# V's products moved between the two groups of a trip's second quarter, in a one-core decode block (attention and feed-forward) on Trainium2

## Chip, core and metric

The kernel runs on one core of one Trainium2 chip. The metric is device time in microseconds (us) of one execution; lower is better. Three executions of the kernel before were timed (median 298.16 us), and a fourth was recorded with the hardware profiler. The engines are called PE (TensorE), DVE (VectorE), ACT (ScalarE), POOL (GpSimd) and SP (SyncE, which issues all large loads here). PEld is PE's weight load.

## The reference, cut to what matters

One decode step for B = 2 sequences, D = 640, 32 heads with head size 192, a key and value cache of 8192 tokens of which the last W = 2048 are used, and a gated feed-forward of width 1536:

```
x = A_x
q = layernorm(x) @ wq
k = k_cache[:, :, Sk - W:, :]
v = v_cache[:, :, Sk - W:, :]
scores = einsum("bhqd,bhkd->bhqk", q, k) * Dh ** -0.5
o = einsum("bhqk,bhkd->bhqd", softmax(scores), v)
h = x + o @ wo
h2 = h + (gelu(layernorm(h) @ w_gate) * (layernorm(h) @ w_up)) @ w_down
```

There is one query per sequence and head, so every key and value is read once and used once: 16 loads of 6.29 MB (8 of K, 8 of V) beside the weights.

## The kernel before, in words

**Storage.** A ring in on-chip memory has three slots of 49152 bytes per partition. A load of K or V (named k0 to k7 and v0 to v7) is one quarter of one sequence's window: 512 tokens for all 32 heads, 128 partitions with 128 tokens each, and fills one slot. Even K loads and v7 use slot 0, odd K loads (and `wq` before them) slot 1, v0 to v6 slot 2. So V has one slot alone: v1 can't be loaded before all reads of v0 are done. `wo` comes into slots 2 and 1 at the end, the feed-forward weights into slots 1 and 0.

**Order of loads.** `load` puts every load into one list, in the order wg0, wq, k0, k1, v0, k2, v1, k3, v2, k4, v3 and so on to v6, v7, wo0 to wo3, the rest. `pump` (called by `done`, when the last reader of a slot has been written into the program) takes them strictly in that order. SP runs them as one queue: each DMA waits until the readers of what lay in its slot have finished, and whatever stands behind it waits too.

**Groups and trips.** The work is 16 groups (g), each half a load. A trip J of the loop (4 trips, looped on PE and DVE, unrolled on ACT and POOL) takes groups 4J to 4J+3: the first quarter (4J and 4J+1) reads load k(2J), the second quarter (4J+2 and 4J+3) reads k(2J+1). For a group:
- `transposes` (L549 to L571): PE transposes K through four PSUM banks, 48 instructions (L560); DVE (L571) and ACT (L569) copy the banks out;
- `scores` (L613 to L622): 24 matmuls (L618) into one bank;
- `softmax` (L626 to L634): DVE takes minus the maximum (L628, L629), ACT the exponentials (L633);
- `e_turn` (L656) and `e_blocks` (L659): DVE turns the exponentials and spreads them into `eblk`, the stationary operand of V's products;
- `pv` (L665 to L683): 64 matmuls (L673) of `eblk` with V, even groups into bank `ops`, odd ones into `m1`. V's load v(2J) belongs to groups 4J and 4J+1, v(2J+1) to 4J+2 and 4J+3.

**Where V's products stand.** They run two groups behind. Those of the first quarter, `pv(4J)` and `pv(4J+1)`, stand in the second quarter of the same trip: behind `maxima()`, that is behind both groups' transposes and scores (L792 to L794). In the program `pv` then has DVE copy the bank to `osb` (L682, L683). Those of the second quarter, `pv(4J+2)` and `pv(4J+3)`, stand in `behind` (L695) in the next trip's first quarter, behind both groups' scores; after the last trip they stand by themselves. After a second quarter `sums` (L643) and `combine` (L685) work out the weights by which partial results are joined; PE's matmuls for it are L644, L687 and L688. In trip 2 `heads_done(0)` (L707) follows `behind`.

Each engine runs its program in order, and all waits are on semaphores; the tables `R`, `W` and `X` of an operation say what it reads, writes, and which PSUM bank it uses.

Of the kernel before, what the change touches and what calls it, by code (L numbers as in the profile page):

```python
# [16 lines left out]
DH = 192  # L17
# [229 lines left out]
def bass_sequential_preLN__sliding_block_cached__geglu_ffn__decode_kernel(  # L247
# [12 lines left out]
    with ExitStack() as ctx:  # L260

        def sb(name, shape, dt):
            return ctx.enter_context(nc.sbuf_tensor(name, shape, dt))

        def ps(name, shape, dt):
            return ctx.enter_context(nc.psum_tensor(name, shape, dt))
# [62 lines left out]
        osb = sb("osb", [128, 2, DH], F32)  # L329
# [19 lines left out]
        ops_ = ps("ops", [128, 512], F32)  # L349
        m1 = ps("m1", [128, 512], F32)  # L350
# [25 lines left out]
        def done(*keys):  # L376
            used.update(keys)
            pump()
# [36 lines left out]
        def dve(fn, R=(), W=(), X=(), cls=1):  # L415
            return P.op("dve", fn, R, W, X, cls=cls if looped else 0)

        def act(fn, R=(), W=(), X=(), cls=0):
            return P.op("act", fn, R, W, X, cls=cls)

        def pe(fn, R=(), W=(), X=(), cls=0):
            return P.op("pe", fn, R, W, X, cls=cls)
# [126 lines left out]
        def transposes(g, lo, hi):  # L549

            kk, ktoks = where["k", g // 2]
            kv = kk.bitcast(F32)
            for n in range(lo, hi):
                c, ch, scalar = TR[n]
                bank, x = tps[n % 4], ("t", n % 4)

                def fn(e, c=c, ch=ch, bank=bank):
                    for u in range(4):
                        off = 6144 * (g % 2) + 128 * (3 * (4 * ch + u) + c)
                        ins = e.transpose(bank[:, 128 * u:128 * (u + 1)], kv[:, off:off + 128], identf[:, :])  # L560
                    return ins

                pe(fn, R=ktoks + ["identf"], X=[x])
                if g % 2 == 1 and n == 11:
                    done(("k", g // 2))
                src = bank.bitcast(BF16)
                dst = ktr[:, c, 1024 * ch:1024 * (ch + 1)]
                if scalar:
                    act(lambda e, dst=dst, src=src: e.activation(out=dst, in_=src, func=ACT.Copy), W=[("kt", n)], X=[x])  # L569
                else:  # L570
                    dve(lambda e, dst=dst, src=src: e.tensor_copy(dst, src), W=[("kt", n)], X=[x], cls=0)  # L571
# [41 lines left out]
        def scores(g):  # L613
            def fn(e):
                for k in range(6):
                    for hg in range(4):
                        cols = ktr[:, k // 2, :].rearrange("p (a x w) -> p a x w", a=16, w=2)[:, :, 32 * hg:32 * (hg + 1), k % 2]
                        ins = e.matmul(sps[32 * hg:32 * (hg + 1), :], lhsT=rq[:, k, hg, :], rhs=cols, start=(k == 0),  # L618
                                       stop=(k == 5), tile_position=(0, 32 * hg))
                return ins  # L620

            pe(fn, R=[("rq", hg) for hg in range(4)] + [("kt", n) for n in range(12)], X=["s"])  # L622
            if g % 4 == 3 and g + 1 < 4 * NQ:
                q_masked((g + 1) // 8)

        def softmax(g):  # L626
            n = g % 4
            dve(lambda e: e.memset(gate[:, :], 0.0), W=["gate"], X=["s"], cls=0)  # L628
            dve(lambda e: e.tensor_tensor_reduce(  # L629
                out=sm[:, :].rearrange("p (u x) -> p u x", x=32), in0=sps[:, :].rearrange("p (u x) -> p u x", x=32),  # L630
                in1=mska[:, :].unsqueeze(1).to_broadcast([128, 16, 32]), scale=-1.0, scalar=2.0 * BIG, op0=ALU.add, op1=ALU.min,
                accum_out=nms[:, n:n + 1]), R=["mska"], W=["sm", ("nm", n)], X=["s"], cls=0)
            act(lambda e: e.activation(out=eexp[:, :], in_=sm[:, :], func=ACT.Exp, bias=nms[:, n:n + 1], scale=-1.0,  # L633
                                       accum_out=zr[:, n:n + 1]), R=[("nm", n), "sm", "gate"], W=["eexp", ("zr", n)])  # L634

        def maxima():
            dve(lambda e: e.tensor_reduce(out=nmin[:, :], in_=nms[:, :], axis=AX.X, op=ALU.min), R=[("nm", k) for k in range(5)],
                W=["nmin"], cls=0)
            dve(ts(mrhs[:, :], oht[:, :], nmin[:, 0:1], ALU.mult), R=["oht", "nmin"], W=["mrhs"], cls=0)
            act(lambda e: e.activation(out=wz[:, 0:5], in_=nms[:, :], func=ACT.Exp, bias=nmin[:, 0:1], scale=-1.0),  # L640
                R=["nmin"] + [("nm", k) for k in range(5)], W=["wz"])
# [14 lines left out]
        def e_turn(g):  # L656
            dve(lambda e: e.transpose(et[:, :], eexp[:, :]), R=["eexp"] + [("eb", 0, 3)] * (g % 2), W=["et"], cls=0)  # L657

        def e_blocks(g):  # L659
            for hg in range(4):  # L660
                dve(lambda e, hg=hg: e.tensor_copy(eblk[32 * hg:32 * (hg + 1), g % 2, :, hg, :],  # L661
                                                   et[32 * hg:32 * (hg + 1), :].rearrange("p (a x) -> p a x", x=32)),
                    R=["et"], W=[("eb", g % 2, hg)], cls=0)

        def pv(g):  # L665
            vv, vtoks = where["v", g // 2]
            bank, x = ((ops_, "o"), (m1, "m1"))[g % 2]

            def fn(e):
                for a in range(16):  # L670
                    for r in range(4):
                        t = 64 * (g % 2) + 4 * a + r
                        ins = e.matmul(bank[32 * r:32 * (r + 1), 0:DH],  # L673
                                       lhsT=eblk[:, g % 2, a, :, :].rearrange("p s x -> p (s x)")[:, r:128:4],
                                       rhs=vv[:, DH * t:DH * (t + 1)], start=(a == 0), stop=(a == 15),
                                       tile_position=(0, 32 * r), skip_group_check=True)
                return ins

            pe(fn, R=[("eb", g % 2)] + [("eb", g % 2, hg) for hg in range(4)] + vtoks, X=[x])
            if g % 2 == 1:  # L680
                done(("v", g // 2))
            if g % 4 < 2:  # L682
                dve(lambda e: e.tensor_copy(osb[:, g % 4, :], bank[:, 0:DH]), W=[("osb", g % 4)], X=[x], cls=0)  # L683

        def combine():  # L685
            def fn(e):
# [8 lines left out]
        def behind(g):  # L695
            dve(ts(osum[:, :], osum[:, :], wp[:, 4:5], ALU.mult), R=["wp", "osum"], W=["osum"], cls=0)
            for k in range(4):
                if k == 2:
                    pv(g)
                    pv(g + 1)  # L700
                src, tok, x = ((osb[:, 0, :], [("osb", 0)], []), (osb[:, 1, :], [("osb", 1)], []), (ops_[:, 0:DH], [], ["o"]),
                               (m1[:, 0:DH], [], ["m1"]))[k]
                dve(lambda e, k=k, src=src: e.scalar_tensor_tensor(out=osum[:, :], in0=src, scalar=wp[:, k:k + 1], in1=osum[:, :],
                                                                   op0=ALU.mult, op1=ALU.add),
                    R=["wp", "osum"] + tok, W=["osum"], X=x, cls=0)
# [67 lines left out]
        for J in range(4):  # L773
            P.loop_seg("a", J)
            for g in (4 * J, 4 * J + 2):
                transposes(g, 0, 12)
                scores(g)
                softmax(g)
                transposes(g + 1, 0, 12)
                scores(g + 1)  # L780
                e_turn(g)
                softmax(g + 1)
                if g % 4 == 0:
                    if J > 0:
                        P.loop_seg("pa", J)
                        behind(g - 2)
                    if J == 2:
                        P.loop_seg("op", J)
                        heads_done(0)
                    P.loop_seg("a2", J)  # L790
                else:
                    maxima()  # L792
                    pv(g - 2)
                    pv(g - 1)  # L794
                e_blocks(g)
                e_turn(g + 1)
                e_blocks(g + 1)
                if g % 4 == 0:
                    P.loop_seg("b", J)
                else:  # L800
                    sums()
                    combine()
# [55 lines left out]
        def rjb(t):  # L858
# [18 lines left out]
            W=[("osb", 0), ("osb", 1)], X=["o"])  # L877
# [60 lines left out]
```

## Time and profile before

| what | value |
|---|---|
| timed executions | 294.39, 298.24, 298.16 us; median 298.16 us |
| the profiled execution | 294.99 us, of which the span of recorded work is 293.7 us |
| granted TensorE clock, mean of the span | 0.853 |
| busy | PE 188.1 us, PEld 155.5 us, DVE 148.0 us, ACT 95.5 us, POOL 23.0 us |
| DMA | 122.46 MB, mean 417 GB/s over the span |
| SP waiting for PE's last product of V (L673, L644 rows) | 110.1 + 79.0 + 8.7 us in the queue's own waits |

In a timeline a row is: start, duration, engine, line, operation, output and input, number of instructions, and in square brackets how long the engine sat idle before it and what it waited for. In a table of stretches a row is: the stretch, its length, busy time of each engine with the number of instructions, the granted TensorE clock (1.00 is full), the mean busy share of the 16 DMA engines and what they moved.

### The profile page before, as it was taken

What the parts mean: (1) busy time and instruction counts of PE and PEld (TensorE: products, weight loads), DVE (VectorE), ACT (ScalarE), POOL (GpSimd) and SP (SyncE); (2) the same over time, 40 slices, a digit from 0 to 9 for tenths busy, and PEclk for the clock granted to TensorE, in tenths of its full rate; (3) what the DMA queues carried; (4) which work ended last, traced back from release to release, by engine and by line L of the source; (5) the groups of instructions that cost most, each with busy time, mean ns of one, the idle gap of its engine ahead of it and who ended that gap; (6) DMA issues with size and microseconds to landing.
All of it is one profiled execution on the core that took longest, in us unless ns stands there. A gap on an engine that the chain in (4) does not pass through costs nothing.

```text
span 293.7 us, 6215 instructions
## 1 busy us (share of the span) xinstructions
PE 188.1 (64%) x2557; PEld 155.5 (53%) x2557; DVE 148.0 (50%) x365; ACT 95.5 (33%) x128; POOL 23.0 (8%) x69
## 2 busy tenths in 40 slices
PE   2007388678848955884788468847881788365385
PEld 1004286476738745763777367637670776352143
DVE  5000036766665673577266746663675266634022
ACT  1001026536506611471266024612650256100001
POOL 8930200000200000002000000020000000000000
PEclk9999959979977996999599959996997599868555
DMA  8999999999889999999999999999999999999994
GB/s 322 486 425 428 424 428 428 424 418 428 353 321 428 428 430 428 428 428 442 442 455 449 428 428 428 428 442 449 428 428 428 428 428 428 428 389 430 423 416 171
DMA packets 4204, 122.46 MB, mean 417 GB/s; under 512 B 478, under 2 KB 608, under 8 KB 1248
## 3 DMA queue, kind: packets, MB, share of 16 engines
q1 hardware_dynamic: 4188, 122.29, 97.0%
q8 instruction: 8, 0.13, 0.2%
q14 instruction: 4, 0.03, 0.0%
q10 hardware_dynamic: 4, 0.00, 0.0%
HBM read 122.29 MB, written 0.00 MB: 416 GB/s over the span
## 4 chain that ended last, share of the span: by engine, by line
DMA 56%; PE 29%; issue 6%; ACT 3%; DVE 3%; SPq 1%; DVEq 0%
DMA ring<-in_A_k_cache_dram 48%; PE tpp L560 19%; DMA ring<-in_A_wo_dram 9%; PE sps L618 3%; PE m L673 2%; PE ops L673 2%; ACT ktr L569 2%; ACT eexp L633 1%; DVE ktr L571 1%; SPq L374 1%; DVE sm L629 1%; PE sps L837 1%; PE m L886 1%; PE m L738 1%; PE ops L837 1%
## 5 line engine op out<-in xcount | busy, mean ns | idle before, releaser
L560 PE MATMUL tpp<-identf,ring 128*128 128x128 f32 x768 | 107.4, 307 | 36.6 <-DMA ring<-in_A_k_cache_dram 30.5
L560 PEld LDWEIGHTS tpp<-identf,ring 128*128 128x128 f32 x768 | 100.1, 160 | 45.6 <-DMA ring<-in_A_k_cache_dram 31.6
L571 DVE COPY ktr<-tpp 128x1024 bf16<-128x1024 bf16 x112 | 77.0, 691 | 54.8 <-PE tpp L560 53.7
L569 ACT ACTIVATE ktr<-tpp 128x1024 bf16<-128x1024 bf16 x80 | 77.4, 1020 | 75.0 <-PE tpp L560 75.0
L618 PE MATMUL sps<-ktr,rq 128*32 128x512 bf16 x384 | 25.2, 390 | 13.7 <-DVE ktr L571 13.7
L633 ACT ACTIVATE eexp<-sm,nms 128x512 bf16<-128x512 f32 x16 | 11.6, 723 | 41.1 <-DVE nms L629 41.1
L618 PEld LDWEIGHTS sps<-ktr,rq 128*32 128x32 bf16 x384 | 10.3, 94 | 24.0 <-ACT ktr L569 17.5
L434 POOL TENSOR_TENSOR rq<-qs,mask 128x192 bf16<-128x192 bf16 x16 | 7.8, 519 | 167.7 <-PE sps L618 154.7
L629 DVE CUSTOM_DVE_ANT_1 sm<-sps,mska 128x512 f32<-128x512 f32 x16 | 11.0, 687 | 16.4 <-issue 16.3
L661 DVE COPY eblk<-et 32x512 bf16<-32x512 bf16 x64 | 18.2, 284 | 2.0 <-DVE nms L629 0.2
L580 PE MATMUL tpp<-ring,xnT 128*32 128x384 bf16 x80 | 5.3, 443 | 15.3 <-DMA ring<-in_A_wq_dram 15.3
L673 PE MATMUL ops<-ring,eblk 128*32 128x192 bf16 x512 | 13.7, 261 | 2.1 <-DMA ring<-in_A_v_cache_dram 2.1
L673 PEld LDWEIGHTS ops<-ring,eblk 128*32 128x32 bf16 x512 | 12.9, 112 | 3.2 <-DMA ring<-in_A_v_cache_dram 2.2
L687 PE MATMUL m<-wz,rowperm 128*128 128x6 f32 x8 | 2.4, 369 | 17.2 <-DVE wz L434 17.2
L673 PE MATMUL m<-ring,eblk 128*32 128x192 bf16 x512 | 12.7, 249 | 0.0
L580 PEld LDWEIGHTS tpp<-ring,xnT 128*32 128x32 bf16 x80 | 2.9, 127 | 17.4 <-issue 15.4
L657 DVE STREAM_TRANSPOSE et<-eexp 128x512 bf16<-128x512 bf16 x16 | 11.3, 706 | 1.0
L673 PEld LDWEIGHTS m<-ring,eblk 128*32 128x32 bf16 x512 | 11.7, 109 | 0.0
L687 PEld LDWEIGHTS m<-wz,rowperm 128*128 128x128 f32 x8 | 2.0, 312 | 17.6 <-DVE wz L434 17.6
L603 DVE CAST qs<-ops 128x384 bf16<-128x384 f32 x1 | 0.6, 557 | 21.3 <-PE ops L598 21.3
L738 PE MATMUL m<-ring,ot 128*2 128x320 bf16 x96 | 6.3, 423 | 6.6 <-DMA ring<-in_A_wo_dram 6.6
L824 ACT ACTIVATE lnv<-tpp,eps_t 98x1 f32<-98x1 f32 x1 | 0.3, 261 | 28.4 <-PE tpp L822 28.4
(144 smaller groups left out, 101.3 us busy)
## 6 DMA issues: line engine op xcount, KB each, us to landing
ring<-in_A_k_cache_dram SPq DMA_DIRECT2D x8, 6144.0 KB, 34.9
ring<-in_A_v_cache_dram SPq DMA_DIRECT2D x8, 6144.0 KB, 22.4
ring<-in_A_wq_dram SPq DMA_DIRECT2D x1, 7680.0 KB, 21.3
ring<-in_A_wo_dram SPq DMA_DIRECT2D x4, 1920.0 KB, 19.2
ring<-in_B_w_gate_dram SPq DMA_DIRECT2D x1, 1536.0 KB, 28.7
ring<-in_B_w_up_dram SPq DMA_DIRECT2D x1, 1536.0 KB, 31.9
ring<-in_B_w_down_dram SPq DMA_DIRECT2D x1, 960.0 KB, 25.5
ring<-in_B_w_down_dram SPq DMA_DIRECT2D x1, 480.0 KB, 26.4
```

Source lines behind the costliest of these rows:

```text
L434: return lambda e: e.tensor_tensor(out=out, in0=a, in1=b, op=op)
L560: ins = e.transpose(bank[:, 128 * u:128 * (u + 1)], kv[:, off:off + 128], identf[:, :])
L569: act(lambda e, dst=dst, src=src: e.activation(out=dst, in_=src, func=ACT.Copy), W=[("kt", n)], X=[x])
L571: dve(lambda e, dst=dst, src=src: e.tensor_copy(dst, src), W=[("kt", n)], X=[x], cls=0)
L580: ins = e.matmul(tps[0][32 * r:32 * (r + 1), 0:384], lhsT=xnT[:, c, 32 * J:32 * (J + 1)], rhs=wq[:, c, 1536 * J + 384 * r:1536 * J + 384 * ...
L618: ins = e.matmul(sps[32 * hg:32 * (hg + 1), :], lhsT=rq[:, k, hg, :], rhs=cols, start=(k == 0), stop=(k == 5), tile_position=(0, 32 * hg))
L629: dve(lambda e: e.tensor_tensor_reduce(out=sm[:, :].rearrange("p (u x) -> p u x", x=32), in0=sps[:, :].rearrange("p (u x) -> p u x", x=32) ...
L633: act(lambda e: e.activation(out=eexp[:, :], in_=sm[:, :], func=ACT.Exp, bias=nms[:, n:n + 1], scale=-1.0, accum_out=zr[:, n:n + 1]), R=[( ...
L657: dve(lambda e: e.transpose(et[:, :], eexp[:, :]), R=["eexp"] + [("eb", 0, 3)] * (g % 2), W=["et"], cls=0)
L661: dve(lambda e, hg=hg: e.tensor_copy(eblk[32 * hg:32 * (hg + 1), g % 2, :, hg, :], et[32 * hg:32 * (hg + 1), :].rearrange("p (a x) -> p a ...
L673: ins = e.matmul(bank[32 * r:32 * (r + 1), 0:DH], lhsT=eblk[:, g % 2, a, :, :].rearrange("p s x -> p (s x)")[:, r:128:4], rhs=vv[:, DH * t ...
L738: ins = e.matmul(m1[32 * r:32 * r + 2, 192:512], lhsT=ot[:, J, kk, :], rhs=wo[:, kk, 320 * h:320 * (h + 1)], start=(J == 0 and kk == 1), s ...
```

## The change

`pv` no longer has DVE copy its bank; a new `o_rows(g)` does that. In the second quarter of every trip `pv(g - 2)` and `pv(g - 1)` move from behind `maxima()` to the place behind `softmax(g)`, ahead of `transposes(g + 1)`. Where they stood the two copies (`o_rows`) remain, so DVE's order of work is the same. `behind` is as before, but for the copies, which it never had (`g % 4` is 2 or 3 there). No instruction is added or removed.

```
             if g % 2 == 1:
                 done(("v", g // 2))
-            if g % 4 < 2:
-                dve(lambda e: e.tensor_copy(osb[:, g % 4, :], bank[:, 0:DH]), W=[("osb", g % 4)], X=[x], cls=0)
+        def o_rows(g):
+            bank, x = ((ops_, "o"), (m1, "m1"))[g % 2]
+            dve(lambda e: e.tensor_copy(osb[:, g % 4, :], bank[:, 0:DH]), W=[("osb", g % 4)], X=[x], cls=0)
...
                 softmax(g)
+                if g % 4 == 2:
+                    pv(g - 2)
+                    pv(g - 1)
                 transposes(g + 1, 0, 12)
...
                     maxima()
-                    pv(g - 2)
-                    pv(g - 1)
+                    o_rows(g - 2)
+                    o_rows(g - 1)
                 e_blocks(g)
```

## The prediction, as it was put on record

> **What bounds the kernel now.** I read the page's DMA row first, then the timeline of SP (when loads are issued), then PE's timeline (when it waits for them).
>
> ```profile
> q1 hardware_dynamic: 4188, 122.29, 97.0%
> ```
> ```profile
> 81.34 0.54 SPq L374 DMA_DIRECT2D ring<-in_A_v_cache_dram  x1
> 81.92 0.60 SPq L374 DMA_DIRECT2D ring<-in_A_k_cache_dram  x1
> 107.89 0.54 SPq L374 DMA_DIRECT2D ring<-in_A_v_cache_dram  x1
> ...
> 221.25 1.18 SPq L374 DMA_DIRECT2D ring<-in_A_v_cache_dram  x2
> ```
> ```profile
> 85.72 0.59 PE L687 MATMUL m<-wz,rowperm 128*128 128x6 f32 x2 [4.31 <-DVE wz L434]
> ...
> 86.59 7.78 PE L560 MATMUL tpp<-identf,ring 128*128 128x128 f32 x48
> ...
> 113.44 8.01 PE L560 MATMUL tpp<-identf,ring 128*128 128x128 f32 x48 [5.64 <-DMA ring<-in_A_k_cache_dram]
> ...
> 142.50 7.16 PE L560 MATMUL tpp<-identf,ring 128*128 128x128 f32 x48 [2.06 <-DMA ring<-in_A_k_cache_dram]
> ...
> 200.61 7.12 PE L560 MATMUL tpp<-identf,ring 128*128 128x128 f32 x48 [2.05 <-DMA ring<-in_A_k_cache_dram]
> ...
> 229.68 7.92 PE L560 MATMUL tpp<-identf,ring 128*128 128x128 f32 x48 [8.51 <-DMA ring<-in_A_k_cache_dram]
> ...
> 258.75 2.76 PE L673 MATMUL ops<-ring,eblk 128*32 128x192 bf16 x64 [2.14 <-DMA ring<-in_A_v_cache_dram]
> 261.29 1.79 PE L673 MATMUL m<-ring,eblk 128*32 128x192 bf16 x64
> ...
> 266.90 0.98 PE L738 MATMUL m<-ring,ot 128*2 128x320 bf16 x24
> ...
> 278.02 1.77 PE L738 MATMUL m<-ring,ot 128*2 128x320 bf16 x24 [2.74 <-DMA ring<-in_A_wo_dram]
> ```
>
> The queue that carries the loads is busy for 97%, and PE waits for K in every quarter from 113.44 on. K loads land at 142.50 (k4), 200.61 (k6) and 229.68 (k7): (229.68 - 142.50) / 3 = 29.06 us for a pair, one V and one K, so 14.53 us a load. That is the pace of the DMA, and what follows the last `wo` landing (278.02) hangs on it. The pace is kept only if a new pair is issued before the old one has landed. V has one slot, so the pair's V is issued when the products with the V before it are done. That lead is 113.44 - 107.89 = 5.6 us for v2 and 229.68 - 221.25 = 8.4 us for v6. Only the first pair has no lead:
>
> ```profile
> 80.50:82.50 2.00, 0.91 (x39) 0.68 (x27) 1.09 (x4) 0.00 (x0) 0.21 (x1) 1.00 0.00 0
> ```
> ```profile
> 80.00:80.50 0.50, 0.50 (x36) 0.50 (x29) 0.36 (x1) 0.45 (x3) 0.50 (x2) 1.00 0.13 33
> ```
>
> The last bytes of k2 move at about 80.4, then nothing moves until past 82.5. v1 and k3, issued at 81.34, bring k3 at 113.44, 32.1 us later: an issue into an empty queue costs 3.0 us over the pace. Without the gap k3 could be there at 80.4 + 29.06 = 109.46, that is 3.98 us earlier. This is the most that earlier products of V can bring.
>
> **The change part by part.**
>
> ```profile
> 60.64 7.13 PE L560 MATMUL tpp<-identf,ring 128*128 128x128 f32 x48 [3.72 <-issue]
> 68.63 1.51 PE L618 MATMUL sps<-ktr,rq 128*32 128x512 bf16 x24 [0.86 <-DVE ktr L571]
> 70.07 2.40 PE L560 MATMUL tpp<-identf,ring 128*128 128x128 f32 x20
> 72.83 3.36 PE L560 MATMUL tpp<-identf,ring 128*128 128x128 f32 x28 [0.36 <-ACT ktr L569]
> 77.04 1.61 PE L618 MATMUL sps<-ktr,rq 128*32 128x512 bf16 x24 [0.86 <-DVE ktr L571]
> 78.38 1.52 PE L673 MATMUL ops<-ring,eblk 128*32 128x192 bf16 x62
> ...
> 79.78 1.52 PE L673 MATMUL m<-ring,eblk 128*32 128x192 bf16 x62
> ```
> ```profile
> 80.03 0.36 DVE L683 COPY osb<-ops 128x192 f32<-128x192 f32 x1 [0.16 <-PE ops L673]
> 81.35 0.36 DVE L683 COPY osb<-m 128x192 f32<-128x192 f32 x1 [0.96 <-PE m L673]
> ```
> ```profile
> 22.58 5.28 PE L580 MATMUL tpp<-ring,xnT 128*32 128x384 bf16 x80 [15.32 <-DMA ring<-in_A_wq_dram]
> ...
> 37.92 8.22 PE L560 MATMUL tpp<-identf,ring 128*128 128x128 f32 x48 [6.23 <-DMA ring<-in_A_k_cache_dram]
> ```
>
> *Trip 0, the products.* Scores of group 2 end at 68.63 + 1.51 = 70.14. Is v0 there? Loads land one after the other: `wq` at 22.58, k0, next in the queue, 15.3 us later. So v0, second behind k0, lands at about 37.9 + 2 x 14.53 = 67.0: no wait, 3 us to spare. The 128 matmuls take 81.30 - 78.65 = 2.65 us, so v1 is issued at about 72.8 instead of 81.34, 7.6 us ahead of the end of k2. SP's order stays V, then K; k3 waits for the transposes of group 3. The gap at 80.5 goes: -3.98 us, up to k3.
>
> *Trip 0, what is pushed back.* Behind the products stand group 3's transposes: 48 at the pace of the row with 20 in 2.40 us, 5.76 us, to 78.6 (before they ended at 76.2, with 0.36 us of waits). Then the last copy (0.86) and the scores (1.6) end at 81.05, 2.4 us later than the 78.65 of before. DVE's chain from there to PE's L687 took 85.72 - 78.65 = 7.07 us, and two waits for the products in it (0.16 + 0.96) go: 5.95 us, so L687 runs at 87.0 and the next trip's transposes, 0.87 behind it, at 87.9 (before 86.59). POOL's masks for the next quarter come 2.4 us later too, and the first scores that need them stand behind the 7.78 us of transposes at 86.59. The copies of `o_rows` keep their place and cost nothing new.
>
> *Trip 1, what is late next.* From 86.59 to the issue of v2 were 107.89 - 86.59 = 21.3 us, PE's own work. Now v2 is issued at 87.9 + 21.3 = 109.2. With the gap gone, k3 lands at 109.46. So the gap of before returns one pair later: the queue is empty once more, and 3.0 us are paid again. k4 lands at 109.2 + 3.0 + 29.06 = 141.3 instead of 142.50. Of 3.98 us there remain 1.2.
>
> *Later second quarters.* v2 lands half a pair earlier than k4, at 126.7. Scores of group 6 end near 109.5 + 5.76 + 2.45 = 117.7, so PE now stands at the products and waits some 9 us for V, with group 7's transposes queued behind them, and their copies on DVE and ACT. What was hidden behind K's transfer (products ready at 130.8, V there before) becomes one cycle, V landed to V landed. Products after such a wait run as at 258.75: 261.29 + 1.79 - 258.75 = 4.33 us, against 2.65. Then transposes 5.76, copy and scores 2.45, DVE's chain 6.0, L687 and L688 0.87, the next first quarter up to V's next issue 21.0 (between 21.3 above and 221.25 - 200.61 = 20.6 in trip 3), refill and landing 3.0 + 14.53. Sum 57.9 us, against 2 x 29.06 = 58.1 us of DMA for the same loads. The two are equal within my working; with a lead of only 58.1 - 57.9 + 3.0 = 3.2 us the queue nearly runs dry each time, and I put 0.25 us on each of the two cycles left (bounds: nothing, and 3 us where the queue is quite empty).
>
> *The end.* v6 lands at 258.75 - 14.53 - 0.7 = 243.5. Products, transposes, scores, chain and combine add 4.33 + 5.76 + 2.45 + 6.0 + 0.87 = 19.4, then group 14's and 15's products 4.33 and the way to the first L738 266.90 - 263.08 = 3.8: 271.0. Three of the four L738 blocks at 1.8 us at most end at 276.4, and the last `wo` lands at 278.02 - 0.7 = 277.3. Hidden, by 0.9 us.
>
> *Sum.* -3.98 + 2.8 (gap returned) + 0.5 = -0.7 us. The profiled execution took 294.99 us (span 293.7, 1.3 around it), so 294.3 by its own measure. The median of the timed runs stands 3.2 us higher; two of three are near 298.2. Nothing in the sum tells which of the two levels the changed kernel meets; I forecast against the median: 298.16 - 0.7 = 297.5.
>
> *A page against a row.* The refill of 3.0 us is from the rows at 81.34 and 113.44. The Trainium skill, "DMA: Bandwidth & Descriptors", section "Anatomy of one DMA", gives about 2.0 us of fixed cost beside bytes over 436 GB/s. It speaks of another path of issue, and the trace here shows 1 us more; by 2.0 the refill would be 1.0 us cheaper in trip 1 and no pair behind would be late, an estimate of 296.0.
>
> **Rivals.**
>
> *The whole gap is won.* If V's next issue comes some 4 us earlier than I add up (DVE's chain shorter, the first quarter 20.6 or less), the queue never empties: -3.98, 294.2 against the median (291.0 by the profiled one). For it: the cycle needs little more lead. Against: 21.3 us was measured in this very trip, and k3's landing moves towards PE.
>
> *TensorE's clock makes the loop PE's.* This is the side on which it gets slower.
>
> ```profile
> 117.00:118.00 1.00, 1.00 (x7) 1.00 (x6) 0.00 (x0) 0.85 (x1) 0.00 (x0) 0.50 1.25 541
> ```
>
> After its wait PE works at clock 0.50 until past 118, over 4 us into its work at 113.44. I let the clock come back within the products, as at 258.75. If it stays down through products and transposes, the products take 2 x 2.54 = 5.1 us and the transposes 8.0 (row 113.44) instead of 5.76: 3.0 us more a cycle, 60.9 against 58.1. Two cycles cost 2 x 2.8 = 5.6 us, and at the end 3.0 less the 0.9 hidden: 2.1. 298.16 - 1.2 + 5.6 + 2.1 = 304.7. It decides from some 0.2 us of extra work a cycle on. Against it: at 261.29 the second 64 products already took 1.79. The Trainium skill, "TensorE: Matmul & The Clock Gate", section "HAM oscillation", says that PE gaps over about 3.4 us bring the half clock back at every tile; the 9 us wait of this change is such a gap, and before the products there was none.
>
> *V lands later than mid-pair.* If the two loads of a pair moved side by side, V would land near its K. Products in second quarters then wait up to 10 us longer. The bound is the trace: v7 was there by 258.75, products with v6 ran before that without a wait. `wq` and k0, 15.3 us apart, speak against it. At 4 us of lateness two cycles cost 8 us: 306.
>
> *Nothing moves.* v0 late at 70.14 by more than 5 us: then v1 goes out no earlier than before, 298.2.
>
> **How the numbers follow.** Forecast (two equal cycles, within 2 us of 297.5) 0.57; whole gap won 0.15; clock, wholly or in part (299.7 to 304.7) 0.18; V late 0.06; nothing moves 0.04. About 2% is what a measurement of this kernel can tell from no change: 292.2 and 304.1. Faster needs the whole gap and runs on the lower level: 0.05. Slower needs the clock's full price or V late: 0.13. Same 0.82. The range reaches from the whole gap on the lower level, rounded in, to the clock's partial price: 292.0 to 303.0; the forecast's own range is 295.5 to 299.5, and 292 to 296 should the runs fall on the lower level.
>
> **What would show it.** v1 issued near 72.8 and no stretch without DMA at 80.5; v2 issued near 109, with a new stretch of little traffic there; second-quarter products in trips 1 to 3 that wait for V (5 to 10 us) and then take over 4 us; V issues 57 to 59 us apart. I am wrong if v1 isn't early, if the products wait for nothing, or if these cycles are over 60 us.

## The result and the profile after

| | kernel before | kernel changed |
|---|---|---|
| median of timed executions | 294.38 us (22 of them, 292.44 to 298.24) | 300.0 us (22, 295.5 to 305.49) |
| ratio to before, with its 95% interval | 1 | 1.012 [1.0094, 1.0146] |
| profiled execution (its span) | 294.99 us (293.7) | 299.04 us (297.7) |
| granted TensorE clock, mean of the span | 0.853 | 0.875 |

The ratio leaves out each kernel's slow executions, and so is smaller than that of the plain medians. Forecast was -0.7 us, no change that could be measured; the kernel is 1.2% slower, some 3.5 us, and the profiled pair differs by 4.05 us. The timed executions spread over 10 us, those of before over 5.8. That 300.0 lies near the forecast 297.5 and inside 292 to 303 is luck: the forecast started from 298.16, the median of three executions, and the median of 22 is 294.38. From there the same -0.7 us would have given 293.7.

First the chain of work that ended last, by engine, of the kernel before and then of the changed one:

```profile
DMA 56%; PE 29%; issue 6%; ACT 3%; DVE 3%; SPq 1%; DVEq 0%
```
```profile
DMA 38%; PE 38%; issue 11%; DVE 8%; ACT 2%; SPq 1%; DVEq 0%
```

Before, the path to the end was mostly transfers. Now PE has as large a share as the DMA, and "issue", time in which an engine waits for nothing that the profile shows, has nearly doubled. The same chain of the changed kernel, in order of time (start, duration, what), shows where:

```profile
73.50 2.98 issue
...
114.15 17.39 DMA ring<-in_A_v_cache_dram
...
171.78 18.99 DMA ring<-in_A_v_cache_dram
...
229.75 19.25 DMA ring<-in_A_v_cache_dram
```

From 114.15 on there is a closed loop, V's load, PE's work, V's next load. Ahead of it, in trip 0, PE stands for 2.98 us. Now the rows that answer to those of the prediction: the load queue's share, SP's issues, PE's timeline.

```profile
q1 hardware_dynamic: 4188, 122.29, 96.2%
```
```profile
77.36 0.54 SPq L374 DMA_DIRECT2D ring<-in_A_v_cache_dram  x1
84.02 0.54 SPq L374 DMA_DIRECT2D ring<-in_A_k_cache_dram  x1
114.15 0.53 SPq L374 DMA_DIRECT2D ring<-in_A_v_cache_dram  x1
...
229.75 1.18 SPq L374 DMA_DIRECT2D ring<-in_A_v_cache_dram  x2
```
```profile
60.47 8.27 PE L560 MATMUL tpp<-identf,ring 128*128 128x128 f32 x48 [4.02 <-issue]
69.59 1.53 PE L618 MATMUL sps<-ktr,rq 128*32 128x512 bf16 x24 [0.86 <-DVE ktr L571]
70.95 1.50 PE L673 MATMUL ops<-ring,eblk 128*32 128x192 bf16 x64
72.27 1.24 PE L673 MATMUL m<-ring,eblk 128*32 128x192 bf16 x49
76.48 0.83 PE L673 MATMUL m<-ring,eblk 128*32 128x192 bf16 x15 [2.98 <-issue]
77.25 6.74 PE L560 MATMUL tpp<-identf,ring 128*128 128x128 f32 x48
84.85 1.60 PE L618 MATMUL sps<-ktr,rq 128*32 128x512 bf16 x24 [0.86 <-DVE ktr L571]
...
92.57 0.60 PE L688 MATMUL m<-wz,rowperm 128*128 128x6 f32 x2 [4.31 <-DVE wz L434]
...
131.58 2.76 PE L673 MATMUL ops<-ring,eblk 128*32 128x192 bf16 x64 [6.76 <-DMA ring<-in_A_v_cache_dram]
134.12 1.61 PE L673 MATMUL m<-ring,eblk 128*32 128x192 bf16 x64
...
175.18 1.97 PE L560 MATMUL tpp<-identf,ring 128*128 128x128 f32 x16 [1.05 <-DMA ring<-in_A_k_cache_dram]
...
190.81 1.52 PE L673 MATMUL ops<-ring,eblk 128*32 128x192 bf16 x64 [2.22 <-DMA ring<-in_A_v_cache_dram]
...
234.54 8.27 PE L560 MATMUL tpp<-identf,ring 128*128 128x128 f32 x48 [4.88 <-DMA ring<-in_A_k_cache_dram]
...
249.04 1.52 PE L673 MATMUL ops<-ring,eblk 128*32 128x192 bf16 x64 [3.83 <-DMA ring<-in_A_v_cache_dram]
```

v1 goes out at 77.36, 4.0 us earlier than before (81.34), but not at the forecast 72.8: within the moved products PE stops for 2.98 us after 64 + 49 matmuls. v2 goes out at 114.15, 6.3 us later than before. In the stretches (us, busy time of PE, PEld, DVE, ACT, POOL, granted clock, DMA share, GB/s):

```profile
73.50:76.50 3.00, 0.02 (x5) 0.01 (x4) 0.00 (x0) 0.00 (x0) 0.00 (x0) 0.97 1.20 513
76.50:78.00 1.50, 1.50 (x19) 1.20 (x19) 0.00 (x0) 0.00 (x0) 0.00 (x0) 0.50 1.14 492
...
110.00:115.00 5.00, 5.00 (x161) 4.50 (x154) 3.33 (x11) 0.82 (x2) 0.00 (x0) 1.00 0.01 2
```

While PE stands, nothing else computes and the DMA runs full. Then PE goes on at half clock. And for 5 us, 110 to 115, nothing is loaded at all: the gap that the change was to remove at 80.5 has come back one pair later, and longer. The view of DMA queues shows what arrives during the stop (queue, kind: packets, MB, share), here between 74 and 75 us, in the changed kernel and then in the one before:

```profile
q8 instruction: 1, 0.02, 6.5%
```
```profile
q8 instruction: 1, 0.02, 6.2%
```

Both fetch a packet of instructions then. The view doesn't say for which engine; the experiments show that PE waits for it. Before, PE reaches that place in its program at some 79 us (an estimate, by counting matmuls) and does not notice; the changed kernel is there at 73.5.

### The profile page after: what moved, and what is told of

Its sections match the earlier page's. It is cut to its first block, busy times and chain, and to the rows that moved or that the text cites. A ratio compares the mean times of both kernels' runs of the same rounds, so it can differ in the third digit from the quotient of the medians.

```text
span 297.7 us, 6207 instructions
## 1 busy us (share of the span) xinstructions
PE 186.9 (63%) x2557; PEld 154.6 (52%) x2557; DVE 147.8 (50%) x365; ACT 96.0 (32%) x128; POOL 22.9 (8%) x69
## 4 chain that ended last, share of the span: by engine, by line
DMA 38%; PE 38%; issue 11%; DVE 8%; ACT 2%; SPq 1%; DVEq 0%
PE tpp L560 25%; DMA ring<-in_A_v_cache_dram 19%; DMA ring<-in_A_k_cache_dram 12%; DMA ring<-in_B_w_down_dram 8%; PE ops L673 5%; PE m L673 4%; PE sps L618 3%; DVE eblk L661 2%; DVE et L657 2%; DVE ktr L571 1%; ACT ktr L569 1%; ACT eexp L633 1%; DVE osb L684 1%; PE m L688 1%; PE m L689 1%
## 5 line engine op out<-in xcount | busy, mean ns | idle before, releaser
L560 PE MATMUL tpp<-identf,ring 128*128 128x128 f32 x768 | 106.0, 305 | 24.1 <-DMA ring<-in_A_k_cache_dram 13.0
L569 ACT ACTIVATE ktr<-tpp 128x1024 bf16<-128x1024 bf16 x80 | 77.6, 1021 | 89.0 <-PE tpp L560 87.7
L673 PE MATMUL ops<-ring,eblk 128*32 128x192 bf16 x512 | 14.7, 276 | 12.8 <-DMA ring<-in_A_v_cache_dram 12.8
L618 PEld LDWEIGHTS sps<-ktr,rq 128*32 128x32 bf16 x384 | 10.1, 94 | 24.3 <-ACT ktr L569 17.5
L673 PE MATMUL m<-ring,eblk 128*32 128x192 bf16 x512 | 13.8, 261 | 3.0 <-issue 3.0
L580 PE MATMUL tpp<-ring,xnT 128*32 128x384 bf16 x80 | 4.7, 409 | 15.2 <-DMA ring<-in_A_wq_dram 15.2
L673 PEld LDWEIGHTS m<-ring,eblk 128*32 128x32 bf16 x512 | 12.4, 113 | 3.2 <-issue 3.2
L739 PE MATMUL m<-ring,ot 128*2 128x320 bf16 x96 | 4.6, 340 | 4.2 <-DMA ring<-in_A_wo_dram 4.2
```

Source lines behind the costliest of these rows:

```text
L580: ins = e.matmul(tps[0][32 * r:32 * (r + 1), 0:384], lhsT=xnT[:, c, 32 * J:32 * (J + 1)], rhs=wq[:, c, 1536 * J + 384 * r:1536 * J + 384 * ...
L673: ins = e.matmul(bank[32 * r:32 * (r + 1), 0:DH], lhsT=eblk[:, g % 2, a, :, :].rearrange("p s x -> p (s x)")[:, r:128:4], rhs=vv[:, DH * t ...
```

## The experiments

Three theories were set against each other. **A**: the loss is made in trip 0, by PE's stop, and the empty queue at 110 follows from it. **B**: it is made in the later trips, where products now wait for V and the loop is too long. **C**: a part of B, TensorE's half clock after those waits. All ratios are against the kernel before; all medians are in us.

**Trip 0 alone, and the later trips alone.** In the first of two kernels the products stand early in trip 0 only, in the second in trips 1 to 3 only; segments of the loop's body are skipped for it.

```
                 if g % 4 == 2:
-                    pv(g - 2)
-                    pv(g - 1)
+                    if J == 0:
+                        P.loop_seg("e", J)
+                        pv(g - 2)
+                        pv(g - 1)
+                    P.loop_seg("b2", J)
...
                     maxima()
+                    if J > 0:
+                        P.loop_seg("l", J)
+                        pv(g - 2)
+                        pv(g - 1)
+                    P.loop_seg("b3", J)
```

(The second kernel has the two conditions exchanged.)

> The products stand between the two groups in trip 0 only; trips 1 to 3 have them where they were before. Theory A (the loss is made in trip 0: TensorE is pushed back there by some 6 us, so v2 is issued only after k3 has landed, and the queue runs dry once, for about 5 us at 110 to 115): 297.5 to 300 us, with v1 issued near 77 and v2 near 114, no wait of TensorE for V in trips 1 to 3. Theory B (the loss is made by the waits for V and the half clock behind them in trips 1 to 3): 292 to 295 us.

Measured: 298.01 (12 executions), ratio 1.0086 [1.0047, 1.0125]. v1 was issued at 79.06, v2 at 115.60, and the stop within the products was 2.85 us. No product of the loop's later trips waited for V, and still most of the loss was there: for A. Not all of it comes from the moved products, though: the stop ahead of group 2's transposes, which PE meets before them, was 5.03 us here and 4.02 in the changed kernel, and the trace is of an execution of 300.83 us.

> The products stand between the two groups in trips 1 to 3 only; trip 0 is as before. Theory A: 293 to 296 us; v1 near 81.3 and v2 near 108 as before, then waits for V of 4 to 8 us in the second quarters, with v3 to v6 issued at least 3 us before the K of the pair before lands. Theory B: 297 to 300 us.

Measured: 302.81 (6), ratio 1.027 [1.0221, 1.0318]. It separates nothing. Skipping code in trip 0 made a new stop:

```profile
75.13 8.38 PE L560 MATMUL tpp<-identf,ring 128*128 128x128 f32 x48 [4.97 <-issue]
```

so v1 went out at 88.70 instead of 81.34, worse than before. The profile shows nothing that this stop waits for; it stands where PE jumps over 128 matmuls. A packet of instructions is counted at 72.5 us, 2.6 us before PE goes on, which speaks for an instruction fetch here too.

**Products behind the second transposes.**

```
+                transposes(g + 1, 0, 12)
                 if g % 4 == 2:
                     pv(g - 2)
                     pv(g - 1)
-                transposes(g + 1, 0, 12)
                 scores(g + 1)
```

> The products stand behind the second group's transposes and ahead of its scores, in all trips. Theory A: v1 goes out near 79 (2.4 us earlier than before), and the scores of group 3 come only about 1.8 us later while DVE's chain is 1.1 us shorter, so v2 goes out near 108.6, still ahead of k3 at about 111: 291.5 to 294 us. Theory B (products ahead of the scores have to wait for V in later trips and lengthen the cycle): 296 to 299 us.

Measured: 294.97 (12), ratio 1.0022 [0.999, 1.0054]. v1 was issued at 80.93, not near 79, because here too the products met a stop:

```profile
78.55 0.28 PE L673 MATMUL ops<-ring,eblk 128*32 128x192 bf16 x3 [2.75 <-issue]
```

v2 was issued at 110.50 and k3 landed at 113.25, so nothing was gained; but nothing was lost either, and no products in the loop's later trips waited for V.

**Fewer bytes in front of the fetch.** If the stop is an instruction packet that stands behind data, it must go when k2's load is almost nothing. Of k2 only 1 of 128 tokens is loaded; the rest of that slot is stale, so the whole time isn't comparable.

```
         def load_k(i):
-            load(("k", i), K_AT[i % 2], SLOT, kv_src(A_k_cache, i), lambda v: v, f"k{i % 2}")
+            n = 1 if i == 2 else TPG
+            load(("k", i), K_AT[i % 2], SLOT, kv_src(A_k_cache, i)[:, :, 0:n * DH], lambda v: v, f"k{i % 2}")
```

> The changed kernel, but load k2 moves only the first of its 128 tokens per partition (31/32 and more of 6.29 MB are left out), so that few bytes are under way between about 67 us and v1; groups 4 and 5 work on what lay in the slot. Only trip 0 is read. If TensorE's stop of 2.98 us within the products of trip 0 is a fetch of instructions that stands behind the data packets, it shrinks to under 1.5 us or goes, and v1 is issued 2 us earlier, near 75. If the stop has another cause (clock, a wait on another engine), it stays near 3 us.

Measured: 295.39 (one execution). PE's timeline:

```profile
68.77 1.51 PE L674 MATMUL ops<-ring,eblk 128*32 128x192 bf16 x64
70.09 1.63 PE L674 MATMUL m<-ring,eblk 128*32 128x192 bf16 x64
71.65 5.57 PE L561 MATMUL tpp<-identf,ring 128*128 128x128 f32 x48
```

The stop is gone. The products take 2.95 us and the transposes 5.57, the forecast's sizes; the packet of instructions came between 68 and 69 us and none between 74 and 75. v1 was issued at 71.75, v2 at 107.42. A's cause of the stop holds: with hardly any data under way the packet comes 5 us sooner and PE doesn't stop. Whether the packet stands behind the data or shares the DMA engines with it, the run doesn't tell.

**The loop turned.** The 4.02 us stop ahead of the transposes at 60.47 (3.72 before) stands where PE jumps over the segments that the first trip leaves out. With the first quarter of trip 0 ahead of the loop, and a second quarter and the next first quarter as its body, that jump is gone. (A run below, with the code shifted, shows that the jump alone isn't the cause.) It was done for the kernel before, for the changed one, and for the place behind the second transposes.

```
+        first(0)
         for J in range(4):
-            P.loop_seg("a", J)
-            for g in (4 * J, 4 * J + 2):
...
+            P.loop_seg("b", J)
+            second(4 * J + 2)
+            if J < 3:
+                P.loop_seg("a", J)
+                first(4 * J + 4, J)
...
-        order = ["a", (0, None, ["pa"]), (1, 3, ["op"]), "a2", "b"]
+        order = ["b", (None, 3, ["a", "pa", (0, 2, ["op"]), "a2"])]
```

> The kernel before with its loop turned: group 0's and 1's part is written ahead of the loop, and the body starts with the second quarter and goes on to the next trip's first quarter, so that in trip 0 TensorE no longer jumps over instructions ahead of the second quarter. Order of all work as before. Theory A (TensorE's stops for instructions in trip 0 make it late there): the 3.7 us ahead of group 2's transposes go, v1 is issued near 77.6 instead of 81.3, the queue runs dry for less, 290.5 to 293 us. Theory B (later waits for V): says nothing of this kernel; no gain without the stop would be 294.

Measured: 293.98 (12), ratio 0.9984 [0.9959, 1.001]. The jump's stop went, but PE then waited 2.79 us for DVE's copies at the same place, and v1 went out at 79.98, not 77.6. No difference.

> The changed kernel (products between the groups of the second quarter in all trips) with the same turned loop. Theory A: v1 near 69 to 71, v2 near 106 to 108, ahead of k3, no stretch without DMA at 110; 291 to 294 us, within 1 us of the kernel before with the turned loop. Theory B (waits for V in trips 1 to 3 cost some 3 us however trip 0 goes): at least 3 us slower than the kernel before with the turned loop, 295 or more.

Measured: 300.41 (6), ratio 1.0162 [1.0111, 1.0213]. PE's timeline of this kernel:

```profile
75.02 6.58 PE L560 MATMUL tpp<-identf,ring 128*128 128x128 f32 x43 [2.98 <-issue]
...
130.18 2.76 PE L673 MATMUL ops<-ring,eblk 128*32 128x192 bf16 x64 [5.30 <-DMA ring<-in_A_v_cache_dram]
...
191.12 2.09 PE L673 MATMUL ops<-ring,eblk 128*32 128x192 bf16 x64 [2.49 <-DMA ring<-in_A_v_cache_dram]
...
251.91 2.76 PE L673 MATMUL ops<-ring,eblk 128*32 128x192 bf16 x64 [8.88 <-DMA ring<-in_A_v_cache_dram]
```

This miss taught most. v1 went out at 71.39, earlier than the prediction had hoped, and it gained nothing: the stop had only moved on, into the transposes behind the products, and v2 still went out at 112.71, into an empty queue. So it isn't v1's time that counts but v2's. And the later cycles, products to products, were 191.12 - 130.18 = 60.9 us and 60.8 us: theory B's loss is real too, and A alone falls.

> Products behind the second group's transposes and ahead of its scores, in all trips, with the turned loop. Theory A: v1 near 75, v2 near 103, 6 us ahead of k3 at 109.5, the queue never dry: 289.5 to 291.5 us, the best of the three. Theory B: not better than the kernel before with the turned loop.

Measured: 293.47 (12), ratio 0.9948 [0.9917, 0.9978], faster than both kernels. SP's and PE's timelines and the stretch:

```profile
76.30 0.53 SPq L374 DMA_DIRECT2D ring<-in_A_v_cache_dram  x1
...
106.50 0.53 SPq L374 DMA_DIRECT2D ring<-in_A_v_cache_dram  x1
```
```profile
112.04 8.17 PE L560 MATMUL tpp<-identf,ring 128*128 128x128 f32 x48 [5.63 <-DMA ring<-in_A_k_cache_dram]
```
```profile
108.00:110.00 2.00, 0.00 (x0) 0.00 (x0) 1.78 (x5) 0.00 (x0) 0.00 (x0) 1.00 0.83 324
```

Both pairs are issued ahead of the end of the pair before, and the queue never stands still; no later product waits for V except the very last. No stop called "issue" occurs in PE's timeline of this kernel; with the products at the same place and the loop as it was there were two, of 2.58 and 2.75 us. Yet k3 lands only 1.4 us earlier than before, and the last `wo` 1.35 us earlier (276.67 against 278.02). That is what filling the gap was worth here.

**The code shifted, the clock kept up, and both.** 47 small idle matmuls ahead of the loop move the places at which instruction blocks end; 12 idle float matmuls ahead of the products, in trips 1 to 3, fill the wait for V.

```
         keep_busy(10)
+        pad(47)
         looped.append(True)
```
```
                 if g % 4 == 2:
+                    if J > 0:
+                        P.loop_seg("w", J)
+                        stay_warm(12)
+                    P.loop_seg("b2", J)
                     pv(g - 2)
```

> The changed kernel with 47 idle small matmuls ahead of the loop, in the 6 us in which TensorE waits for k0 anyway; they move the places at which TensorE has to fetch the next 16 KB of instructions 47 matmuls forward, out of the end of trip 0's products. Theory of the fetch: the stop of 2.98 us in trip 0's products goes (or falls under 1 us), v1 is issued near 74, v2 near 110 instead of 114, the stretch without DMA at 110 shrinks from 5 us to about 2, and the time is 2 to 4 us under the changed kernel's: 296 to 298. If the stop does not hang on where the code lies: v2 stays near 114 and the time at 299 to 301.

Measured: 296.9 (12), ratio 1.0075 [1.0043, 1.0108], between the two kernels. PE's and SP's timelines:

```profile
62.25 5.20 PE L560 MATMUL tpp<-identf,ring 128*128 128x128 f32 x33 [4.51 <-issue]
...
73.29 1.51 PE L673 MATMUL m<-ring,eblk 128*32 128x192 bf16 x62 [2.01 <-issue]
...
127.61 2.76 PE L673 MATMUL ops<-ring,eblk 128*32 128x192 bf16 x64 [6.89 <-DMA ring<-in_A_v_cache_dram]
```
```profile
110.11 0.53 SPq L374 DMA_DIRECT2D ring<-in_A_v_cache_dram  x1
```

The stop in the products now comes after 64 + 2 of their matmuls instead of 64 + 49: 47 earlier, exactly as many as were put in front. So where it falls is set by a place in the program and not by the data that PE works on. The stop ahead of group 2's transposes has moved too: PE passes the jump, does 15 transposes (55.88 to 57.74) and then stands for 4.51 us. So there also the place of the code counts, and a jump by itself need not cost a stop. The stop in the products is 2.01 us, v2 goes out 4.0 us earlier, and V's products of trip 1 start at 127.61 instead of 131.58.

> The changed kernel with 12 idle f32 matmuls of TensorE (128x128, into an unused part of a PSUM bank) ahead of the second quarter's products, in trips 1 to 3 only; they run while V is awaited. Theory of the clock (after the wait for V the products run at half clock, 4.2 to 5.1 us instead of 2.8, and the cycle from V to V is 59 to 61 us instead of 58.1): the products after the wait take under 3.2 us, the two cycles 58.0 to 58.6 us, and the time falls from the changed kernel's 300.0 median to 296.5 to 299. If the clock is not what lengthens the cycles: 59 us or more a cycle with warm products, 299 to 303. Trip 0 stays as in the changed kernel (v2 near 114).

Measured: 300.36 (6), ratio 1.014 [1.0087, 1.0192]. Rests of 3.94, 2.14 and 2.20 us remained between the idle matmuls and the products, and these still ran at half clock, so this run doesn't test the theory of the clock. The added code also moved trip 0's stop (4.05 us).

> Both of them together: shifted code and 12 idle matmuls ahead of the products in trips 1 to 3. If these two are the whole of the loss against my sum, the time comes down to that of the kernel before, 293.5 to 296; if something else takes part, it stays above 297.

Measured: 297.98 (12), ratio 1.0089 [1.0055, 1.0123], so not the time of the kernel before: the two insertions together place the stops anew (2.26 and 0.58 us), and v2 went out at 112.25 (in an execution of 299.71 us).

> As the kernel kept warm, with 20 idle matmuls instead of 12 ahead of the products in trips 1 to 3, so that TensorE's rest before V lands is under some 2 us. In seven traces so far a cycle from V to V took 57.7 to 58.7 us (3 cycles) where the products at its start ran at the full clock, and 58.3 to 61.3 us (11 cycles) where they ran at half. Theory of the clock: products under 3.2 us and cycles of 58 to 59 us here, so that the end comes 166 to 167 us after v2 lands. If products run at the full clock and the cycles still take 60 us or more, the clock is not the cause. Products that still run at half clock leave it open. Trip 0 is left as in the changed kernel, so the time as a whole is read only beside that: 296 to 300 us.

Measured: 299.52 (4), ratio 1.0169 [1.012, 1.0218]. With 20 idle matmuls:

```profile
132.50 1.52 PE L673 MATMUL ops<-ring,eblk 128*32 128x192 bf16 x64 [2.17 <-DMA ring<-in_A_v_cache_dram]
...
191.90 1.52 PE L673 MATMUL ops<-ring,eblk 128*32 128x192 bf16 x64
...
250.55 1.52 PE L673 MATMUL ops<-ring,eblk 128*32 128x192 bf16 x64 [1.49 <-DMA ring<-in_A_v_cache_dram]
```

All products are at full clock; the cycles are 59.4 and 58.65 us, shorter than the 60.9 and 60.8 of the turned kernel, but not shorter than the 59.2 and 58.2 of the changed kernel, from which this one differs only by the idle matmuls. From v2's products to the span's end are 166.4 us here and 166.1 there. So a gain from the full clock isn't shown. Nor is it ruled out: the products at 191.90 waited for no data, because the idle matmuls ran until then and may have held them up. Trip 0 was worse here (v2 at 115.00, its stop 5.02), so the time as a whole tells nothing of it either.

**V in two halves**, so that the slot's first half comes free after one group, in the best kernel.

```
         def load_v(i):
-            load(("v", i), V_AT if i < 2 * NQ - 1 else 0, SLOT, kv_src(A_v_cache, i), lambda v: v, f"v{i % 2}")
+            for h in range(2):
+                load(("v", i, h), (V_AT if i < 2 * NQ - 1 else 0) + h * SLOT // 2, SLOT // 2,
+                     kv_src(A_v_cache, i)[:, :, h * TPG // 2 * DH:(h + 1) * TPG // 2 * DH], lambda v: v, f"v{i % 2}{h}")
```

> The best kernel so far (products behind the second transposes and ahead of the second scores, turned loop; ratio 0.995) with each V load cut in two, one per group, so that the first half of the next V can be issued when the even group's products are done, 1.3 us sooner. If the lead of V's issue over the landing of the K before it is still short (5.5 us for v2, with a dip to 324 GB/s at 108 to 110 us), this fills the dip: another 0.3 to 1 us, ratio 0.991 to 0.995. If the queue is full already: the same, 0.994 to 0.997.

Measured: 293.43 (12), ratio 0.9968 [0.9951, 0.9985], the same as without halves. v1 was issued at 75.49, v2 at 104.44, and k3 landed at 111.16: an issue still earlier is worth little once the queue never runs dry.

## Why the prediction was wrong, step by step

**The bound before** was read rightly: the DMA with one dry stretch. But the ceiling of 3.98 us was mis-sized. It was worked out from the moment when all transfers of k2 had ended (80.4) and a pace of 29.06 us a pair. In the two kernels where no gap remains, k3 lands at 112.04 and 111.16 against 113.44: 1.4 to 2.3 us. Summing the DMA's rates over the stretches of the traces gives 46.1 MB moved by 111.8 us in the kernel before and by 108.5 us in the first of these two, 3.3 us sooner (an estimate). So the transfers were ahead by most of the ceiling, but k3's landing by 1.4 us only; what the difference is made of stays open.

**Trip 0, the products**: this is the step that failed. It had PE at 70.14 at the products and 2.65 us for them, from a row in which they ran at 78.65, over 4 us behind the packet of instructions counted at 74.1; it put the fetch of them at nothing. Measured: there at 71.12, and 77.31 - 71.12 = 6.2 us, of which 2.98 are the stop and 0.6 the half clock behind it (0.50 from 76.48 to 77.31). The 1.0 us at the start arose ahead of the moved products: group 2's transposes took 8.27 us here and 7.13 before. The prediction quoted the 3.72 us "issue" in its own row at 60.64 and didn't ask what it was. It is the same kind of stop, and a first sign that PE still had to fetch the loop's code in this trip; in no later trip of either kernel does PE stop that way.

**Trip 0, what is pushed back**: transposes 6.74 us for 5.76, with the clock at half up to about 79.5; scores end at 84.85 + 1.60 = 86.45, forecast 81.05. DVE's chain to the first product of `combine` took 92.57 - 86.45 = 6.12 us against 5.95, as forecast, and so its two waits went.

**Trip 1**: the mechanism was right, that the gap returns one pair later through v2. The first quarter took 114.15 - 93.45 = 20.7 us for 21.3 (the transposes start 0.88 behind the row at 92.57). v2 came 114.15 - 109.2 = 4.95 us later than forecast: 1.0 late at the products, 3.5 in them, 1.0 in the transposes, 0.2 in the chain, -0.6 in the quarter, which makes 5.1. From v2's issue to its products were 131.58 - 114.15 = 17.4 us, forecast 3.0 + 14.53 = 17.5. The refill of 3.0 us, read from the trace before, held.

**Later cycles**: forecast 58.1 + 0.25 us each. In the profiled execution they were 59.2 and 58.2, 1.2 us over two DMA cycles where 0.5 had been charged. In the turned kernel they were 60.9 and 60.8, the 60.9 us of the rival "TensorE's clock makes the loop PE's". So cycles of the length that this rival gave do occur, but that the clock makes them isn't shown.

In the changed kernel, the turned one, and those with shifted code, 12 and 20 idle matmuls, six cycles that begin with products at half clock (59.2, 60.9, 60.8, 60.0, 60.5, 58.3) have a mean of 59.95 us, and four that begin at full clock (58.2, 58.7, 59.4, 58.7) one of 58.74. The cycles left out here, of the kernel with both insertions, the one with later trips only and the one with little of k2, lie on the same sides (59.6 to 61.3 at half clock, 57.7 at full). The Trainium skill, "TensorE: Matmul & The Clock Gate", section "HAM oscillation", has the half clock return after idle gaps of over 3.4 us. The traces agree on the large waits (6.76 us, then 2.76 for 64 products) but not near the limit, where 3.83 us was followed by full clock and the 2.20 us rest of an experiment by half.

The lead is a second candidate. In the changed kernel the pair issued at 171.78, 3.4 us before K's landing at 175.18, brought its V only at 190.81, 1.1 us after 175.18 + 14.53; the one issued at 229.75, 4.8 us ahead of 234.54, lost nothing (249.04). But a short lead need not cost that much: with the products behind the second transposes, v2 went out 2.75 us ahead of k3's landing (110.50 and 113.25), and k4 landed at 142.54, only 0.2 us later than the pace. How much of each loss is clock and how much the short lead stays open, since a slower cycle also shortens the lead, and the runs with idle matmuls don't part them.

**The end**: hidden, as forecast. From V's products at 249.04 to the span's end are 48.7 us; the forecast's 243.5 and 293.0 make 49.5.

**The sum** for the profiled pair: 4.9 us for v2, 0.7 more in the two cycles, 0.8 less at the end, 4.8 in all, against 297.7 - 293.0 = 4.7 measured. In this execution nearly the whole miss is trip 0's. Why the timed ones reach from 295.5 to 305.49 isn't shown, since only one of them left a trace; those of the best placing without halves stay within 292.71 to 294.57.

**The rivals.** "The whole gap is won" failed with v2, "V lands later" and "nothing moves" did not occur: v2 was there 17.4 us after its issue, as forecast, v0 was there at 70.95 without a wait, and v1 was early.

## What to carry to other kernels

Where a load has one slot, it is the next issue but one that decides: an early issue which pushes back what frees the slot again only moves the gap, so leave a lead well over the refill cost in every cycle (the refill was 3 us here, and the best placing issued v2 5.5 us ahead). A stop called "issue" on the first pass through a piece of code is a cost of its own: dense instructions that are moved ahead in time lose the cover under which their code was fetched, so take their duration from a first pass, not from a warm row. The place one step later, behind the second transposes, with a loop that needs no jump in its first trip, gave 0.5%; either of the two alone gave nothing that could be measured (ratios 1.0022 and 0.9984).

## What the runs showed of the hardware

- PE's stop is the fetch of its own instructions. It is tied to a place in the program (47 matmuls put in front, 47 matmuls earlier), and it goes when hardly any data is under way. Eight kernels (the changed one and seven experiments) stop in this stretch of straight code. In all eight PE goes on 2.2 to 2.6 us behind the tenth of a microsecond in which the view counts an instruction packet, although the stops are from 2.0 to 5.0 us long. In the kernel with little of k2 the packet is counted at 68.8 us, and PE reaches the place only near 71 (an estimate). Such stops occurred in trip 0 alone; in the changed kernel no packet of that queue is counted between 84 and 250 us. The Trainium skill, "Runtime: NRT & Kernel Launch", section "Instruction fetch mechanics", says that code is fetched in blocks of 16 KiB, that crossing a block is mostly hidden, and that a taken branch to code outside the two current blocks forces a fetch. The traces agree on the size (0.02 MB a packet), and on the branch only in part: 3.72 and 4.02 us ahead of the transposes at 60 us were gone with the turned loop, but with 47 matmuls in front PE passed the jump and stopped behind it. On straight code with the DMA at 513 GB/s the measured 2.98 us wasn't hidden.
- Every insertion of code moved these stops or changed their length, by up to microseconds. An experiment that adds instructions changes trip 0 as well, so read its trace there before its time.
- After the stop of 2.98 us PE ran at clock 0.50 (76.5 to 78 us): here a stop for code was followed by the half clock as long waits for data were.
